# Three value turns a head instead of four, more of the feed-forward's products inside attention, and its weight tiles in two pools

## The chip, the core and the metric

The kernel runs on one core of one Trainium2 chip. The metric is the device time of one execution in microseconds (us), lower is better. An execution's profile names the engines PE (TensorE's matmuls), PEld (its weight loads, which lie beside them), DVE (VectorE), ACT (ScalarE), POOL (GpSimd) and SP (the engine that issues nearly all DMAs here).

## The reference

A block of attention and a gated feed-forward read the same x (2048 rows of 448), and a sigmoid gate per row mixes them. There are 16 heads of 28, and F is 1792.

```python
def _A_ref(x, wqkv, wo):
    qkv = (x @ wqkv).reshape(B, S, 3, H, Dh).transpose(2, 0, 3, 1, 4)
    q, k, v = qkv[0], qkv[1], qkv[2]
    scores = jnp.einsum("bhqd,bhkd->bhqk", q, k) * (Dh ** -0.5)
    p = _softmax(scores, axis=-1)
    o = jnp.einsum("bhqk,bhkd->bhqd", p, v)
    return o.transpose(0, 2, 1, 3).reshape(B, S, D) @ wo

def _B_ref(x, w_gate, w_up, w_down):
    return (_gelu(x @ w_gate) * (x @ w_up)) @ w_down

g = _sigmoid((x * gate_w).sum(-1, keepdims=True))
return g * a + (1 - g) * b
```

All is float32. A product that needs the full width is made of a high and a low part of each operand; 448 rows then take 11 matmuls of 128 rows (the list PAIRS).

## The kernel before

It has three stages, with PE's matmuls in the order in which they are written (`mm` pins each behind the one before). The other engines' instructions, DMA issues too, are ordered by a planner from its own estimate of when each is ready, except where they are pinned.

The first stage makes Q and K (tiles `pqk`, stored to `qkd`) and V with the gate column (`pv`).

**Attention** goes head by head, and in a head over 16 tiles `kt` of 128 keys. `scores` makes for each `kt` two score tiles (`half` 0 and 1): two matmuls into an `sc` tile of 1024 columns (three buffers), then one exponential on ACT into a `pt` tile (12 buffers). `values` multiplies V with the `pt` tiles of one `kt` into `po`, one PSUM bank, in column groups of 32, so that four matmuls stand side by side in the array. The values of several `kt` are done together as a turn: `ENDS` names the `kt` after which a turn's tiles are complete, and the turn's `values` follow `LATE` score tiles later. Between score tiles `fill` takes steps from the generator `up` (line 338): each step is one of the 11 matmuls of a tile `pu`, first for x @ w_up of all 14 tiles of F, then for x @ w_gate of the first `NB` tiles. A finished tile is copied by DVE (L352) to `u` and stored to `ud`. There is one `pu` bank, so after a finished tile `fill` gives nothing until `hold` is counted down by one per score tile, or a turn of values clears it. `RATE` says how many steps follow a score tile; in the first turn of the first head and the last of the last it is 4, and none follow the tile just before a turn's values. What is left at the end of the heads is done behind the last values (line 406). The weights' halves for it are loaded and split by `load_half`.

After a head's last values `finish` (line 319) copies `po` to `o`, sends its row of sums through DRAM (`dend`, `r`, `rdend`, `rb`), multiplies, and stores to `od`: four transfers one behind another, all on SP's queue.

**The last stage** goes over F in chunks of two tiles (`ORDER` lists chunks) and in each over four blocks of 512 rows (`tb`). `hidden` loads `u`, gets x @ w_gate either from DRAM (`gs`, for the first `NB` tiles of F) or by 11 matmuls `pg`, and makes the hidden tile `hl2` by gelu, product, and high and low parts on ACT and DVE. `down` multiplies the block before with w_down, 24 matmuls `pd`, and DVE adds them into `acc`. PE's order is: the `pg` of one block, then `down` of the block before it. `load_f` loads w_down's rows for one tile of F and splits them into a tile `w0`, `w1` or `w2`, in rotation (L431, L432). In chunks 2 and 3 the attention's output is loaded (`load_o`) and multiplied with wo (`project`).

On-chip memory is a stack of pools from the left, and one from the right for pools with `side="right"`. A pool that takes over memory of a closed one waits until that is free: as a whole, or tile by tile where it says `reuse_waits="tile"`. Before the change `w0`, `w1`, `w2` and `draw` lie in one pool `gp` on the right, opened ahead of attention.

Of the kernel before, what the change touches and what calls it, by code (L numbers as in the profile page):

```python
# [7 lines left out]
F32 = mybir.dt.float32  # L8
F32R = mybir.dt.float32r
# [7 lines left out]
S, D, H, DH, F = 2048, 448, 16, 28, 1792  # L17
P = 128
TB = 512
# [3 lines left out]
NQK = 2 * D // P  # L23
NF = F // P
FC = 2
ENDS = (3, 7, 11, 15)
LATE = 3
RATE = 2
NB = 3
ORDER = (2, 3, 1, 4, 0, 5, 6)  # L30
AHEAD = 8
WARM = 9
LAG = 6
# [12 lines left out]
def gated_mix(ctx: ExitStack, tc: tile.TileContext, xT, wqk, wvg, wg, wu, wd, wo, sel, ident, out):  # L46
# [12 lines left out]
    rdend = dram.tile([H, S], F32, name="rdend")  # L59
    ud = dram.tile([NF + NB, P, S], F32, name="ud")  # L60

# [22 lines left out]
    with ExitStack() as ph:  # L84
# [87 lines left out]
        def v_tile(i):  # L172
            p = psv.tile([P, VW], F32, name="pv")
            for j, (x, w) in enumerate(PAIRS):
                m = mm(p, X[:, x, i * P:(i + 1) * P], WV[:, w, :], j == 0, j == len(PAIRS) - 1)
            a = pin(nc.scalar.activation(V[:, i, :, 0:DH], p[:, 0:D].rearrange("p (h d) -> p h d", h=H), AF.Copy))
            d = pin(nc.vector.tensor_copy(gate[:, 0, i:i + 1], p[:, D:D + 1]))
            return m, a, d
# [30 lines left out]
        for i in range(4, NT):  # L209
            last = v_tile(i)  # L210
# [40 lines left out]
    with tc.If(bounded < 1, label="rows"):  # L251
        with ExitStack() as ph:
            gp = ph.enter_context(tc.tile_pool(name="gp", bufs=2))
# [23 lines left out]
                nc.sync.dma_start(out=shd[h].rearrange("a (i n) -> i a n", i=NT),  # L277
                                  in_=ms.bitcast(F32))

    gp = ctx.enter_context(tc.tile_pool(name="gp", bufs=1, side="right"))  # L280
    def by_act(o, i):
        return nc.scalar.activation(o, i, AF.Copy)


    with ExitStack() as ph:
        pp = ph.enter_context(tc.tile_pool(name="pp", bufs=12))
        op = ph.enter_context(tc.tile_pool(name="op", bufs=2))
        psc = ph.enter_context(tc.tile_pool(name="psc", bufs=3, space=PSUM))
        pso = ph.enter_context(tc.tile_pool(name="pso", bufs=1, space=PSUM))
        psu = ph.enter_context(tc.tile_pool(name="psu", bufs=1, space=PSUM))  # L290
        PT, PO = {}, {}

        def load_head(h):
            Q, K = heads[h % 2]
            if h:
                load_k(K, h)
                load_q(Q, h)
            nc.sync.dma_start(out=Q[4 * DH:NR].bitcast(F32), in_=shd[h])

        def scores(h, kt, half):  # L300
            Q, K = heads[h % 2]
            sc = psc.tile([P, 1024], F32, name="sc")
            for c in range(2):
                mm(sc[:, c * 512:(c + 1) * 512], K[:, kt * P:(kt + 1) * P],
                   Q[:, half * 1024 + c * 512:half * 1024 + (c + 1) * 512], True, True)
            pt = pp.tile([P, 1024], F32, name="pt")
            nc.scalar.activation(pt, sc, AF.Exp, scale=SCALE)  # L307
            PT[h, kt, half] = pt

        def values(h, kt):  # L310
            if kt == 0:
                PO[h] = pso.tile([P, 512], F32, name="po")
            for j in range(4):
                mm(PO[h][j * 32:(j + 1) * 32], V[:, kt, h, :],
                   PT[h, kt, j // 2][:, (j % 2) * 512:(j % 2 + 1) * 512], kt == 0, kt == NKT - 1)
            if kt == NKT - 1:
                finish(h)

        def finish(h):
            o = op.tile([P, 512], F32, name="o")  # L320
            nc.vector.tensor_copy(o, PO[h])
            for j in range(4):
                nc.sync.dma_start(out=dend[h:h + 1, j * 512:(j + 1) * 512],
                                  in_=o[j * 32 + DH:j * 32 + DH + 1])
            r = op.tile([P, S // P], F32, name="r")
            nc.sync.dma_start(out=r, in_=dend[h].rearrange("(p n) -> p n", p=P))
            nc.vector.reciprocal(r, r)
            nc.sync.dma_start(out=rdend[h].rearrange("(p n) -> p n", p=P), in_=r)
            rb = op.tile([P, 512], F32, name="rb", bufs=1)
            for j in range(4):  # L330
                nc.sync.dma_start(out=rb[j * 32:(j + 1) * 32],
                                  in_=rdend[h:h + 1, j * 512:(j + 1) * 512].to_broadcast([32, 512]))
            nc.vector.tensor_tensor(o, o, rb, OP.mult)
            for j in range(4):
                nc.sync.dma_start(out=od[h * DH:(h + 1) * DH, j * 512:(j + 1) * 512],
                                  in_=o[j * 32:j * 32 + DH])

        def up():

            todo = [(wu, f, "u") for f in range(NF)] + [(wg, f, "g") for f in range(NB)]  # L340
            for n, (_, f, key) in enumerate(todo):
                for tb in range(NTB):
                    if tb == 1 and 1 < n + 1 < len(todo):
                        load_half(*todo[n + 1], nc.vector.tensor_copy)
                    s = slice(tb * TB, (tb + 1) * TB)
                    p = psu.tile([P, TB], F32, name="pu")
                    for i, (x, w) in enumerate(PAIRS):
                        mm(p, halves[key, f][:, w], X[:, x, s], i == 0, i == len(PAIRS) - 1)
                        if i < len(PAIRS) - 1:
                            yield False  # L350
                    u = op.tile([P, TB], F32, name="u")
                    nc.vector.tensor_copy(u, p)  # L352
                    nc.sync.dma_start(out=ud[n, :, s], in_=u)
                    yield True

        filler = up()

        hold = 0

        def fill(n):  # L360

            nonlocal hold
            while n and not hold:
                n -= 1
                if next(filler, None):
                    hold = 2

        def spaced(h, kt, half):
            nonlocal hold
            scores(h, kt, half)  # L370
            hold = max(hold - 1, 0)

        def gates():

            pin(nc.scalar.activation(gate[:, 0], gate[:, 0], AF.Exp, scale=-1.0))
            nc.vector.tensor_scalar(gate[:, 0], gate[:, 0], 3e38, 1.0, OP.min, OP.add)
            nc.vector.reciprocal(gate[:, 1], gate[:, 0])
            nc.vector.tensor_scalar(gate[:, 2], gate[:, 1], -1.0, 1.0, OP.mult, OP.add)

        load_head(0)  # L380
        fill(11)
        ready, due, count = [], [], 0
        for h in range(H):
            for kt in range(NKT):
                if kt == 2 and h + 1 < H:
                    load_head(h + 1)
                if kt == 2 and h == 1:
                    gates()
                for half in range(2):
                    spaced(h, kt, half)  # L390
                    count += 1
                    if due and count == LATE:
                        for a in due:
                            values(*a)
                        due, hold = [], 0
                    elif count != LATE - 1 or h + kt == 0:
                        first, last = h == 0 and kt <= ENDS[0] + 1, h == H - 1 and kt > ENDS[-2]
                        fill(4 if first or last else RATE)
                ready.append((h, kt))
                if kt in ENDS:  # L400
                    ready, due, count = [], ready, 0
        fill(11)
        for a in due:
            values(*a)
        hold = 0
        while next(filler, None) is not None:
            pass
    attn.close()


    with ExitStack() as ph:
        ap = ph.enter_context(tc.tile_pool(name="ap", bufs=1, reuse_waits="tile"))
        acc = ap.tile([P, NT, D], F32, name="acc")
        hp = ph.enter_context(tc.tile_pool(name="hp", bufs=2, reuse_waits="tile"))
# [6 lines left out]
        def load_f(f):  # L421
            if f >= NB:
                load_half(wg, f, "g", by_act)

            n = len(WD) % 3
            size, hi, lo = ((TB + D, 0, TB), (TB + D, 0, TB), (TB + D + 32, 64, 64 + D))[n]
            w = gp.tile([P, size], F32R, name=f"w{n}", bufs=1)
            draw = gp.tile([P, D], F32, name="draw")
            nc.sync.dma_start(out=draw, in_=wd[f * P:(f + 1) * P])
            hi, lo = w[:, hi:hi + D], w[:, lo:lo + D]  # L430
            nc.scalar.activation(hi, draw, AF.Copy)  # L431
            nc.vector.tensor_tensor(lo, draw, hi.bitcast(F32), OP.subtract)  # L432
            WD[f] = hi, lo

        def hidden(f, tb, hl):
# [3 lines left out]
            g = tp.tile([P, TB], F32, name="g")  # L439
            if f < NB:  # L440
                pg = tp.tile([P, TB], F32, name="gs")
# [62 lines left out]
                    mm(p, O[:, x, i * P:(i + 1) * P], WO[:, w], k == 0, k == len(PAIRS) - 1)  # L504
                nc.vector.scalar_tensor_tensor(acc[:, t], p, gate[:, 1, t:t + 1], acc[:, t], OP.mult, OP.add)

        order = [f for c in ORDER for f in range(c * FC, (c + 1) * FC)]
        load_f(order[0])
        pend = None
        for n in range(NF // FC):  # L510
# [53 lines left out]
```

## Time and profile before

| | |
|---|---|
| median of 3 runs | 1052.24 us (1051.49 to 1052.64) |
| the profiled execution | 1051.69 us |
| its span, first to last instruction | 1049.9 us |
| PE busy in the span | 1041.3 us (99%) |
| ACT busy | 610.5 us (58%) |
| DVE busy | 315.7 us (30%) |
| granted TensorE clock, mean | 1.000 |

The span is what the page and the trace divide up; the rest of the profiled execution lies around it. A line of the timeline gives the start in us, the duration, the engine, the source line and the operation as out<-in, with a count where equal instructions are merged; in square brackets stands the idle time before it and what ended it. All matmuls carry line 52, that of the helper `mm`, so they are told apart by their tiles. A matmul of `po` counts as two instructions. Matmuls are pipelined and a duration reaches into the next one's, so what one costs PE is read from start to start.

### The profile page before, as it was taken

Reading aid. Unit: us, or ns where it says so; the run is one execution under the profiler, and the core shown is the slowest. Engines: PE = TensorE matmul, PEld = TensorE weight load, DVE = VectorE, ACT = ScalarE, POOL = GpSimd, SP = SyncE. Lnnn points to the kernel's source line nnn. Section 1 sums busy time; section 2 is a strip of 40 time slices with the busy share of each in tenths; the row PEclk is TensorE's granted clock in tenths of the full one; section 3 lists DMA queues with packets and bytes.
Section 4 is the critical chain, followed back from the end, with each engine's and each line's share of the span. In section 5 each row is a group of like instructions: output and inputs, shape, how many; then the busy total and the mean of one; then the engine's idle time right before and its main releaser. Section 6 shows DMA issues by size and latency. Waiting matters only on the chain.

```text
span 1049.9 us, 14556 instructions
## 1 busy us (share of the span) xinstructions
PE 1041.3 (99%) x5673; PEld 731.4 (70%) x5673; DVE 315.7 (30%) x512; ACT 610.5 (58%) x732; POOL 51.3 (5%) x38
## 2 busy tenths in 40 slices
PE   9999999999999999999999999999999999999998
PEld 6889765655655656656556556556588898899887
DVE  4552112111111011011011111110157666577555
ACT  5332477877777778778777777787643332233321
POOL 4322000000000000000000000000001011100000
PEclk9999999999999999999999999999999999999999
DMA  7865333332332332332332332331264323242223
GB/s 250 306 253 122 79 94 87 118 104 80 108 95 77 111 95 75 108 101 74 104 105 75 98 110 74 96 109 37 70 190 141 112 80 100 88 150 68 67 86 117
DMA packets 58906, 115.84 MB, mean 110 GB/s; under 512 B 12784, under 2 KB 18160, under 8 KB 55216
## 3 DMA queue, kind: packets, MB, share of 16 engines
q1 hardware_dynamic: 58544, 114.32, 36.2%
q8 instruction: 47, 0.77, 0.3%
q10 hardware_dynamic: 288, 0.52, 0.2%
q14 instruction: 27, 0.22, 0.1%
HBM read 74.44 MB, written 40.37 MB: 109 GB/s over the span
## 4 chain that ended last, share of the span: by engine, by line
PE 88%; ACT 0%; issue 0%; DVE 0%; ACTq 0%
PE sc L52 23%; PE po L52 22%; PE pd L52 16%; PE pu L52 16%; PE pg L52 11%; ACT pt L307 0%; DVE y L470 0%; ACT w L431 0%; ACTq L307 0%
## 5 line engine op out<-in xcount | busy, mean ns | idle before, releaser
L307 ACT ACTIVATE pt<-sc 128x1024 f32<-128x1024 f32 x512 | 477.9, 1040 | 160.7 <-PE sc L52 160.4
L52 PE MATMUL sc<-Q,K 128*128 128x512 f32 x1024 | 313.5, 398 | 1.7 <-issue 1.6
L52 PEld LDWEIGHTS sc<-Q,K 128*128 128x128 f32 x1024 | 187.1, 188 | 91.0 <-issue 54.8
L52 PE MATMUL pu<-X,half 128*128 128x512 f32 x748 | 233.3, 391 | 0.1
L52 PE MATMUL po<-pt,V 128*32 128x512 f32 x2048 | 233.0, 595 | 0.0
L352 DVE COPY u<-pu 128x512 f32<-128x512 f32 x68 | 47.0, 691 | 488.3 <-PE pu L52 477.4
L52 PEld LDWEIGHTS pu<-X,half 128*128 128x128 f32 x748 | 140.1, 188 | 32.4 <-issue 1.4
L52 PEld LDWEIGHTS po<-pt,V 128*32 128x32 f32 x2048 | 60.0, 109 | 138.2 <-issue 132.7
L52 PE MATMUL pd<-w,hl 128*128 128x448 f32 x672 | 140.1, 365 | 0.0
L52 PEld LDWEIGHTS pd<-w,hl 128*128 128x128 f32 x672 | 126.2, 188 | 11.1
L52 PE MATMUL pg<-X,half 128*128 128x512 f32 x484 | 114.0, 390 | 0.0
L52 PEld LDWEIGHTS pg<-X,half 128*128 128x128 f32 x484 | 90.9, 188 | 18.4
L52 PE MATMUL pqk<-X,WQK 128*128 128x512 f32 x308 | 70.9, 391 | 1.0 <-ACT X L143 0.8
L52 PEld LDWEIGHTS pqk<-X,WQK 128*128 128x128 f32 x308 | 57.5, 188 | 14.7 <-ACT X L143 1.5
L447 ACT ACTIVATE g<-pg 128x512 f32<-128x512 f32 x44 | 26.2, 594 | 70.3 <-PE pg L52 70.2
L448 DVE TENSOR_TENSOR g<-g,u 128x512 f32<-128x512 f32 x56 | 46.4, 837 | 50.8 <-ACT g L447 50.7
L449 ACT ACTIVATE hl<-g 128x512 fp32r<-128x512 f32 x56 | 35.2, 631 | 42.2 <-DVE g L448 36.8
L467 DVE SCALAR_TENSOR_TENSOR acc<-pd,gate,acc 128x448 f32<-128x448 f32 x80 | 52.7, 679 | 6.0 <-PE pd L52 5.9
L495 POOL TENSOR_TENSOR ohl<-oraw,ohl 128x1536 fp32r<-128x1536 f32 x4 | 14.0, 3502 | 704.8 <-ACT ohl L491 704.8
L450 DVE TENSOR_TENSOR hl<-g,hl 128x512 fp32r<-128x512 f32 x56 | 38.3, 687 | 10.6 <-ACT hl L449 8.5
L162 ACT ACTIVATE hl<-pqk 128x512 fp32r<-128x512 f32 x28 | 16.7, 598 | 41.6 <-PE pqk L52 39.7
L52 PE MATMUL pv<-WV,X 128*128 128x450 f32 x176 | 36.5, 367 | 0.0
(62 smaller groups left out, 357.0 us busy)
## 6 DMA issues: line engine op xcount, KB each, us to landing
ud<-u SPq DMA_DIRECT2D x68, 256.0 KB
qkd<-hl SPq DMA_DIRECT2D x28, 512.0 KB
K<-qkd SPq DMA_DIRECT2D x64, 224.0 KB
Q<-qkd SPq DMA_DIRECT2D x64, 224.0 KB
u<-ud SPq DMA_DIRECT2D x56, 256.0 KB
rb<-rdend SPq DMA_DIRECT2D x64, 64.0 KB
raw<-in_xT SPq DMA_DIRECT2D x14, 256.0 KB
hraw<-in_wu SPq DMA_DIRECT2D x14, 256.0 KB
```

Of the source, the lines that this page charges most:

```text
L52: return pin(nc.tensor.matmul(o, lhsT, rhs, start=start, stop=stop))
L162: pin(nc.scalar.activation(hl[:, 0], p, AF.Copy))
L307: nc.scalar.activation(pt, sc, AF.Exp, scale=SCALE)
L352: nc.vector.tensor_copy(u, p)
L447: nc.scalar.activation(g, pg, AF.Gelu_apprx_tanh)
L448: nc.vector.tensor_tensor(g, g, u, OP.mult)
L449: nc.scalar.activation(hl[:, 0], g, AF.Copy)
L450: nc.vector.tensor_tensor(hl[:, 1], g, hl[:, 0].bitcast(F32), OP.subtract)
L467: nc.vector.scalar_tensor_tensor(acc[:, t], p, g1, acc[:, t], OP.mult, OP.add)
L495: nc.gpsimd.tensor_tensor(O[:, 4:7], o[:, 0:3], O[:, 0:3].bitcast(F32), OP.subtract)
```

## The change

`ENDS` has three turns a head, of 5, 5 and 6 key tiles, instead of four of 4. `LATE` is 2: a turn's values follow the second score tile behind its end. `RATES` replaces `RATE`, two filler steps for the first six score tiles of a turn and three for the next six, and the tile before the values is no longer left without. `HOLD` counts three score tiles instead of two. `NB` is 6: x @ w_gate of six tiles of F is made in attention, so 20 x 44 filler matmuls instead of 17 x 44. `ORDER` lists tiles instead of chunks: the first chunk has two computed tiles (6, 7), and each of the others one computed and one loaded. There are 14 `pt` tiles and one `o`. `gp` becomes `gp0`, with `w0` and `draw`, and a new pool `gp1` on the right, opened with the last stage, with `w1` and `w2`; the two halves of a weight tile lie at 0 and at 512 in each.

```diff
-ENDS = (3, 7, 11, 15)
-LATE = 3
-RATE = 2
-NB = 3
-ORDER = (2, 3, 1, 4, 0, 5, 6)
+ENDS = (4, 9, 15)
+LATE = 2
+RATES = (2,) * 6 + (3,) * 6
+HOLD = 3
+NB = 6
+ORDER = (6, 7, 8, 0, 9, 1, 10, 2, 11, 3, 12, 4, 13, 5)
...
-    gp = ctx.enter_context(tc.tile_pool(name="gp", bufs=1, side="right"))
+    gp0 = ctx.enter_context(tc.tile_pool(name="gp0", bufs=1, side="right"))
...
-        pp = ph.enter_context(tc.tile_pool(name="pp", bufs=12))
+        pp = ph.enter_context(tc.tile_pool(name="pp", bufs=14))
...
-            o = op.tile([P, 512], F32, name="o")
+            o = op.tile([P, 512], F32, name="o", bufs=1)
...
                 if next(filler, None):
-                    hold = 2
+                    hold = HOLD
...
-                    elif count != LATE - 1 or h + kt == 0:
+                    else:
                         first, last = h == 0 and kt <= ENDS[0] + 1, h == H - 1 and kt > ENDS[-2]
-                        fill(4 if first or last else RATE)
+                        fill(4 if first or last else RATES[count - 1])
...
     with ExitStack() as ph:
+        gp1 = ph.enter_context(tc.tile_pool(name="gp1", bufs=1, side="right"))
         ap = ph.enter_context(tc.tile_pool(name="ap", bufs=1, reuse_waits="tile"))
...
             n = len(WD) % 3
-            size, hi, lo = ((TB + D, 0, TB), (TB + D, 0, TB), (TB + D + 32, 64, 64 + D))[n]
-            w = gp.tile([P, size], F32R, name=f"w{n}", bufs=1)
-            draw = gp.tile([P, D], F32, name="draw")
+            w = (gp1 if n else gp0).tile([P, 2 * TB if n else TB + D + 32], F32R, name=f"w{n}")
+            draw = gp0.tile([P, D], F32, name="draw")
             nc.sync.dma_start(out=draw, in_=wd[f * P:(f + 1) * P])
-            hi, lo = w[:, hi:hi + D], w[:, lo:lo + D]
+            hi, lo = w[:, 0:D], w[:, TB:TB + D]
...
-        order = [f for c in ORDER for f in range(c * FC, (c + 1) * FC)]
+        order = ORDER
```

## The prediction

> **What bounds the kernel now.** I read the page's busy times first, then its chain of work that ended last.
>
> ```profile
> span 1049.9 us, 14556 instructions
> PE 1041.3 (99%) x5673; PEld 731.4 (70%) x5673; DVE 315.7 (30%) x512; ACT 610.5 (58%) x732; POOL 51.3 (5%) x38
> PE sc L52 23%; PE po L52 22%; PE pd L52 16%; PE pu L52 16%; PE pg L52 11%; ACT pt L307 0%; DVE y L470 0%; ACT w L431 0%; ACTq L307 0%
> ```
>
> PE is busy all the time, and the chain is PE from end to end. A change pays only if it takes time from PE's own stream, and costs whatever it leaves PE waiting. So next comes one turn of attention from the timeline (start, duration, engine, line), and busy time by stretch (PE, PEld, DVE, ACT, POOL, granted clock, DMA share, GB/s) for all of attention and for a stretch of the last stage.
>
> ```profile
> 298.84 3.64 PE L52 MATMUL po<-pt,V 128*32 128x512 f32 x32
> 299.29 0.13 PEld L52 LDWEIGHTS po<-pt,V 128*32 128x32 f32 x4 [0.30 <-issue]
> ...
> 301.44 0.13 PEld L52 LDWEIGHTS po<-pt,V 128*32 128x32 f32 x4 [0.30 <-issue]
> 302.41 0.73 PE L52 MATMUL sc<-Q,K 128*128 128x512 f32 x2
> 302.98 0.62 PE L52 MATMUL pu<-X,half 128*128 128x512 f32 x2
> ...
> 307.76 1.08 PE L52 MATMUL sc<-Q,K 128*128 128x512 f32 x4
> 308.77 1.07 PE L52 MATMUL po<-pt,V 128*32 128x512 f32 x8
> ```
>
> ```profile
> 135.00:735.00 600.00, 599.93 (x3558) 358.60 (x3557) 81.19 (x141) 452.57 (x491) 0.00 (x0) 1.00 0.32 92
> 838.00:880.00 42.00, 42.00 (x203) 37.89 (x203) 26.85 (x41) 11.96 (x19) 4.11 (x2) 1.00 0.39 115
> ```
>
> From one po block's start to the next are 9.93 us: 3.57 us of values, then 16 score and 11 pu matmuls. In both stretches PE waits for nobody.
>
> **The turns.** Between 302.98 and 307.76 lie 21 matmuls (11 pu, 10 sc), 0.2276 us each. The first two of the turn take 302.98 - 302.41 = 0.57 us, 0.115 more than 2 x 0.2276. The last four take 308.77 - 307.76 = 1.01 us, 0.10 too much. The values go in eight groups of (301.44 - 299.29) / 5 = 0.43 us, so 3.44 us, and the block lasts 3.57, 0.13 more. One turn thus costs about 0.345 us that is no matmul's own. The change makes 3 turns a head of 4, 48 of 64 in all: 16 x 0.345 = **-5.5 us**. The bounds are nothing, if the 0.345 goes with the value steps, which stay the same in number, and 5.5. I take 5.5, since it sits only at the two seams and both remain as they were.
>
> The Trainium skill (TensorEngine Tiling, Key Properties) says that changing the tiling mode drains TensorE; po runs as 128*32 and the rest as 128*128, and the row's seams agree.
>
> **What the longer turns ask.** Followed through the loop, a turn between values is S uu S uu S uu S uu S uuu S S S, then S with two or three u behind it (S a score tile of two matmuls, u one pu matmul). Up to the eighth S this is the old turn within one matmul, so ACT meets it as before. Its rate and its lag:
>
> ```profile
> 739.47 0.73 PE L52 MATMUL sc<-Q,K 128*128 128x512 f32 x2
> 740.30 7.45 ACT L307 ACTIVATE pt<-sc 128x1024 f32<-128x1024 f32 x8 [1.98 <-PE sc L52]
> L307 ACT ACTIVATE pt<-sc 128x1024 f32<-128x1024 f32 x512 | 477.9, 1040 | 160.7 <-PE sc L52 160.4
> L352 DVE COPY u<-pu 128x512 f32<-128x512 f32 x68 | 47.0, 691 | 488.3 <-PE pu L52 477.4 <-DMA ud<-u 6.8 <-DVEq L251 4.0
> ```
>
> An exponential follows the last by (7.45 - 1.04) / 7 = 0.916 us, and the first starts 0.83 us after its tile. The seventh ends at 0.83 + 6 x 0.916 + 1.04 and 0.2 of waiting for the sixth tile, which has 21 matmuls before it: 7.6 us. The tenth tile, which needs its buffer, starts at 34.5 x 0.2276 = 7.9 us. It fits with 0.3 us to spare: cost nothing, and if it is late it costs the lateness on each of 48 turns. Six steps need 12 pt tiles and two more before the values: the 14 that there are. One psu bank lies idle while DVE copies it (0.69 us); HOLD keeps two or three score tiles over that, or one and the values. One o buffer is enough, since its use below lasts some 24 us of a head's 42 (4 x 9.93, less one seam, and 11 matmuls more).
>
> **The moved products.** Three more tiles of x @ w_gate are 3 x 4 x 11 = 132 matmuls. In attention they cost 0.2276 us, in the last stage 0.228 (9.97 us for 44 below): nothing. Around them go 12 copies of 0.69 us and three weight splits on DVE (81 of 600 us busy in attention), 12 stores and 12 loads of 256 KB more on SP's queue (DMA share 0.32 and 0.39). In the last stage each block of 512 rows has then one pg tile (2.5 us) instead of two. The row 838 to 880 is that case already: one tile computed, one loaded, and PE ran 42.00 of 42.00 us. DVE worked 26.85 of them, so it would need half as much again to become the bound.
>
> **The end of attention.** All 20 x 44 = 880 filler matmuls are used up before the end: behind the values of the last middle turn come S uuuu S uuuu S uuu and then seven S with nothing between, and no filler behind the last values. Three psc buffers let PE run three tiles ahead. The fourth S starts at 19.5 x 0.2276 = 4.4 us, its exponential at 4.7, the seventh tile's at 7.45, and the tenth S waits for that to end at 8.5; it ends at 9.05. Unhindered it would end at 31.5 x 0.2276 = 7.2. So +1.9 us; before, the same stretch (749.41 to 757.06, 7.65 us for 32 matmuls and seams, 7.50) lost 0.15: **+1.7 us**.
>
> **The weights of the second tile.** Here is the step that decides. Before, w0, w1 and w2 had memory of their own through attention:
>
> ```profile
> L431 ACT ACTIVATE w<-draw x14: 562/579/637, 161.2 to 1010.5; 128x448 fp32r<-128x448 f32 x14
> L432 DVE TENSOR_TENSOR w<-draw,w x14: 614/624/626, 161.8 to 1011.1; 128x448 fp32r<-128x448 f32 x14
> 757.06 3.64 PE L52 MATMUL po<-pt,V 128*32 128x512 f32 x32
> 760.63 2.79 PE L52 MATMUL pu<-X,half 128*128 128x512 f32 x11
> 760.77 0.69 DVE L321 COPY o<-po 128x512 f32<-128x512 f32 x1 [2.91 <-PE po L52]
> 761.49 1.12 SPq L323 DMA_DIRECT2D dend<-o  x4
> 763.26 10.14 PE L52 MATMUL pg<-X,half 128*128 128x512 f32 x44
> 765.66 0.32 SPq L326 DMA_DIRECT2D r<-dend  x1
> 769.97 0.33 SPq L328 DMA_DIRECT2D rdend<-r  x1
> 773.23 5.03 PE L52 MATMUL pd<-w,hl 128*128 128x448 f32 x24
> 773.32 1.71 SPq L331 DMA_DIRECT2D rb<-rdend  x4
> 779.26 0.68 DVE L333 TENSOR_TENSOR o<-o,rb 128x512 f32<-128x512 f32 x1
> 779.97 1.65 SPq L335 DMA_DIRECT2D od<-o  x4
> 784.56 0.49 SPq L488 DMA_DIRECT2D oraw<-od  x1
> ```
>
> The first split ran at 161 us. After the change only w0 is there early; w1 and w2 lie in gp1, opened after attention on the right, below gp0. Per partition the left side then reaches 57,568 (keep) + 16,384 (fw) + 32,768 (V) + 32,768 (Q, K) + 57,344 (14 pt) + 8,320 (op) = 205,152 bytes, and gp0 with gp1 takes 13,952 from the top. The kernel before fills 212,448. If that is about all there is, gp1 lies on op's u, o, r and rb, and w1 can't be written until finish(15) is done with them. The two stay apart only if there are 219,104 bytes.
>
> The Trainium skill (SBUF — State Buffer, "SBUF size: 192, 224, or 256?") gives about 208 KiB usable on trn2, 212,992 bytes; no run here shows it, and by it they overlap.
>
> finish(15) took from 760.63, when its values ended, to 784.56, when the first load that needs its store was let go: 23.9 us. PE's first down product stands behind 44 pg matmuls (9.97 us) and reads w1 at its fourth matmul, 0.6 us on: 10.6 us after the values, since no filler lies between them any more. What delayed r before was that filler's store; ACT's and DVE's work hangs on the pg tiles, which come 2.6 us earlier. So the chain shifts to 21.3 us, w1's first half follows 0.6 later (579 ns), and PE waits 21.9 - 10.6 = 11.3 us. Without anything ahead of it in a queue it would be shorter, with the gap from rdend to rb in another head as the landing of each small transfer:
>
> ```profile
> 719.75 0.69 DVE L321 COPY o<-po 128x512 f32<-128x512 f32 x1 [3.83 <-PE po L52]
> 722.51 0.34 SPq L326 DMA_DIRECT2D r<-dend  x1
> 726.32 0.37 SPq L328 DMA_DIRECT2D rdend<-r  x1
> 728.24 1.71 SPq L331 DMA_DIRECT2D rb<-rdend  x4
> ```
>
> r is issued 2.8 us after the copy, and four more landings at 1.9 with the issues of rb and od (1.7, 1.6), DVE's two steps (0.9) and w1's copy (0.6) come to 15.3 us: a wait of 4.7. The upper bound is before's chain unshifted, 24.5 - 10.6 = 14. I take **+10 us**, near the row that is this very chain. Behind the waiting matmul stand all others of PE's queue; ACT and DVE wait for their pg tiles, so nothing is caught up. On ACT the copy into w1 waits too, with the gelus of later tiles behind it; the first four tiles' are ready long before, and I take them as queued ahead of it.
>
> **PE after the rest.** No row shows PE after a rest of 10 us within the kernel. After 1.6 us it loses nothing; from the start of the program it is slow:
>
> ```profile
> 1.47 4.21 PE L52 MATMUL warm<-zero 128*128 128x512 f32 x9 [1.47 <-DVE zero L100]
> 119.12 1.16 PE L52 MATMUL sc<-Q,K 128*128 128x512 f32 x4 [1.62 <-issue]
> 120.14 1.19 PE L52 MATMUL pu<-X,half 128*128 128x512 f32 x4
> ```
>
> Nine matmuls in 4.21 us, against 9 x 0.228 = 2.05. Bounds 0 and 2.2; I take **+2**, since a rest of 10 us is nearer to the first row.
>
> The Trainium skill (TensorE: Matmul & The Clock Gate, Part 1) has the clock at half after an idle window of about 3.4 us and until as long a busy one, which would be some 1.7 us, an estimate; the granted clock in this trace is 1.00 everywhere.
>
> **The sum.** -5.5 + 1.7 + 10 + 2 = +8.2 us. The profiled execution took 1051.69 us (span 1049.9, 1.8 around it), so 1059.9; the median shown is 0.5 above it. I say 1060, with 1052.5 to 1064 for this case from its bounds (wait 4.7 or 14, clock 0 or 2.2).
>
> **Rivals.** *The weights come in time*: gp1 lies free, or w1 is ready within 10.6 us of the last values. Then 1051.7 - 5.5 + 1.7 = 1048, faster. For it: the four landings are short taken singly. Against: the bytes, and the 23.9 us. It decides at 10.6. *The turns save nothing*: the seam's time goes with the value steps; with the wait it is 1065.4, without it 1053.4. Against: the seam stands at the mode's change alone. *Late score tiles*: the exponentials fall behind by 0.1 us more than the 0.3 on every turn, 48 x 0.1 = 5 us on top, 1065.
>
> **Chances.** The wait with the saving 0.64; weights in time 0.22; no saving, with the wait 0.05, without 0.03; late score tiles 0.06. A measurement here tells 0.2%, 2 us, from no change. Of the first case 0.05 falls within 0.2%, with the 0.03 that makes 0.08 for the same, 0.22 faster and 0.70 slower. The range, 1047.5 to 1065, takes in the second case and leaves out the ends beyond the bounds.
>
> **What would show it.** Right: 48 po blocks with the same seams; seven S in pace with ACT before the last; no w of the second tile before op's last store; PE idle 4.7 to 14 us ahead of the fourth pd matmul, released by the split of w. Wrong: an early split of the second w, or pd following pg without a gap; sc waiting for pt on middle turns; PE idle in the last stage's blocks.

## The result, and the profile after

The changed kernel is slower: 1082.38 us, median of 4 runs (1081.75 to 1084.36), against 1051.97 us for the kernel before in the same session (4 runs, 1051.49 to 1052.64). The ratio is 1.029, 95% interval 1.0278 to 1.0302. The forecast was 1060 with a range of 1047.5 to 1065: the sign was right, the size was not.

First the head of the page after, and its chain of work that ended last by engine.

```profile
span 1080.0 us, 14639 instructions
PE 1043.3 (97%) x5673; PEld 735.5 (68%) x5673; DVE 321.0 (30%) x527; ACT 607.8 (56%) x729; POOL 51.0 (5%) x38
...
PE 84%; DMA 2%; DVE 1%; SPq 1%; issue 1%; ACT 0%; DVEq 0%; ACTq 0%
```

Before, the chain was PE from end to end and PE was busy 99% of the span. Now DMA, DVE and SP's queue have entered the chain. PE executes as many matmuls (5673) and is busy only 2.0 us longer, so nearly all of the 30.1 us more span is time in which it stands. The waits of PE (line, releaser: us in total, times, longest) say where:

```profile
PE pd L53 <- ACT w L433: 15.9, 1, 15.9
PE pu L53 <- DVE u L354: 8.8, 3, 3.1
PE pd L53 <- DVE w L434: 2.5, 1, 2.5
...
PE sc L53 <- ACT pt L309: 1.1, 4, 0.6
```

Two kinds of stop were in no row of before: one of 15.9 + 2.5 = 18.4 us at the first down product, which the prediction had foreseen at 10, and three of about 3 us at filler matmuls, which it had not.

The start of the first pg divides the two stages. The timeline of after, around that place:

```profile
801.79 10.27 PE L53 MATMUL pg<-X,half 128*128 128x512 f32 x44
801.92 0.69 DVE L323 COPY o<-po 128x512 f32<-128x512 f32 x1 [9.07 <-PE po L53]
...
807.79 0.32 SPq L328 DMA_DIRECT2D r<-dend  x1
...
811.13 0.33 SPq L330 DMA_DIRECT2D rdend<-r  x1
...
811.89 0.77 PE L53 MATMUL pd<-w,hl 128*128 128x448 f32 x3
...
817.76 1.71 SPq L333 DMA_DIRECT2D rb<-rdend  x4
819.26 2.03 DVE L483 TENSOR_TENSOR WO<-oraw,WO 128x1792 fp32r<-128x1792 f32 x1 [4.23 <-ACT WO L482]
...
821.25 0.69 DVE L335 TENSOR_TENSOR o<-o,rb 128x512 f32<-128x512 f32 x1
821.31 0.38 SPq L488 DMA_DIRECT2D oraw<-od  x1
821.97 1.61 SPq L337 DMA_DIRECT2D od<-o  x4
826.52 1.48 ACT L493 ACTIVATE ohl<-oraw 128x1536 fp32r<-128x1536 f32 x1 [7.29 <-DMA oraw<-od]
...
827.91 0.56 ACT L433 ACTIVATE w<-draw 128x448 fp32r<-128x448 f32 x1
828.13 3.43 POOL L497 TENSOR_TENSOR ohl<-oraw,ohl 128x1536 fp32r<-128x1536 f32 x1 [743.39 <-ACT ohl L493]
828.50 3.55 DVE L434 TENSOR_TENSOR w<-draw,w 128x448 fp32r<-128x448 f32 x1 [6.55 <-ACT w L433]
828.52 1.11 PE L53 MATMUL pd<-w,hl 128*128 128x448 f32 x2 [15.86 <-ACT w L433]
...
832.10 6.43 PE L53 MATMUL pd<-w,hl 128*128 128x448 f32 x19 [2.47 <-DVE w L434]
...
838.37 5.18 PE L53 MATMUL pg<-X,half 128*128 128x512 f32 x22
```

Up to pg the kernel takes 801.79 - 763.26 = 38.5 us more than before. The moved products are 132 x 0.2276 = 30.0 of these, so attention itself has become **8.5 us** slower. From pg to the end it takes 1080.0 - 801.8 = 278.2 us, against 1049.9 - 763.3 = 286.6 less the 30.1 that moved away, 256.5: **21.7 us** slower. The two together are the 30.1, within rounding.

The three-turn schedule itself is visible: blocks of x40, x40 and x48 po instructions a head. At the end of attention come seven score tiles in ACT's pace, as predicted (seven exponentials in 6.51 us from 792.03). The long stop is also where it was predicted: the fourth down matmul waits for the copy of w, and that copy starts only after op's last store. By the profile's chain of work, the last part of that store is issued at 823.20 and lands 4.03 us later, and what releases ACT's copy of w is this landing. But the chain that leads to it (o, dend, r, rdend, rb, o, od, w) takes 26.7 us, from the end of the values at 801.8 to the first half of w at 827.91 + 0.56 = 828.5; the prediction had 21.9. And the three stops within attention are new.

This is one of them, in the timeline of after (PE's other matmuls left out):

```profile
309.17 0.43 DVE L80 CAST half<-hraw 128x512 fp32r<-128x512 f32 x1 [4.64 <-PE pu L53]
...
310.24 0.68 DVE L335 TENSOR_TENSOR o<-o,rb 128x512 f32<-128x512 f32 x1
310.95 1.60 SPq L337 DMA_DIRECT2D od<-o  x4
312.59 0.39 SPq L241 DMA_DIRECT2D Q<-qkd  x1
...
313.33 0.82 SPq L355 DMA_DIRECT2D ud<-u  x2
...
317.03 0.69 DVE L354 COPY u<-pu 128x512 f32<-128x512 f32 x1 [6.11 <-DMA ud<-u]
...
317.78 0.75 PE L53 MATMUL pu<-X,half 128*128 128x512 f32 x2 [3.10 <-DVE u L354]
```

Read it from the bottom. PE waits for the copy of pu, since there is one pu bank. The copy waits for a store of u: there are two u buffers. That store stands on SP's queue behind the stores of od. Those wait for the product of o and rb on DVE, and this stands on DVE behind the split of the next weight half (L80), which waits 4.64 us for PE to read the old half for the last time. Nobody needs that split soon. It is only ahead in the queue.

### The profile page after: what moved, and what is told of

It is laid out like the page before. It is cut to its first block, busy times and chain, and to the rows that moved or that the text cites. A ratio compares the mean times of both kernels' runs of the same rounds, so it can differ in the third digit from the quotient of the medians.

```text
span 1080.0 us, 14639 instructions
## 1 busy us (share of the span) xinstructions
PE 1043.3 (97%) x5673; PEld 735.5 (68%) x5673; DVE 321.0 (30%) x527; ACT 607.8 (56%) x729; POOL 51.0 (5%) x38
## 4 chain that ended last, share of the span: by engine, by line
PE 84%; DMA 2%; DVE 1%; SPq 1%; issue 1%; ACT 0%; DVEq 0%; ACTq 0%
PE sc L53 22%; PE po L53 20%; PE pu L53 19%; PE pd L53 16%; PE pg L53 7%; DMA ud<-u 1%; DMA oraw<-in_wo 1%; SPq L337 1%; DMA od<-o 0%; DVE w L434 0%; DVE o L335 0%; DVE u L354 0%; ACT pt L309 0%; DVE WO L483 0%; ACT WO L482 0%
## 5 line engine op out<-in xcount | busy, mean ns | idle before, releaser
L53 PE MATMUL sc<-Q,K 128*128 128x512 f32 x1024 | 308.3, 398 | 2.6 <-issue 1.5
L53 PE MATMUL pu<-X,half 128*128 128x512 f32 x880 | 260.6, 392 | 9.0 <-DVE u L354 8.8
L53 PE MATMUL po<-pt,V 128*32 128x512 f32 x2048 | 229.7, 594 | 0.0
L354 DVE COPY u<-pu 128x512 f32<-128x512 f32 x80 | 55.3, 692 | 485.0 <-PE pu L53 397.9
L53 PEld LDWEIGHTS pu<-X,half 128*128 128x128 f32 x880 | 165.5, 188 | 46.3 <-DVE u L354 10.1
L53 PE MATMUL pd<-w,hl 128*128 128x448 f32 x672 | 143.9, 370 | 18.3 <-ACT w L433 15.9
L53 PEld LDWEIGHTS pd<-w,hl 128*128 128x128 f32 x672 | 128.2, 191 | 30.9 <-ACT w L433 16.2
L53 PE MATMUL pg<-X,half 128*128 128x512 f32 x352 | 85.0, 391 | 0.0
L449 ACT ACTIVATE g<-pg 128x512 f32<-128x512 f32 x32 | 19.1, 597 | 109.3 <-PE pg L53 109.3
L53 PEld LDWEIGHTS pg<-X,half 128*128 128x128 f32 x352 | 66.0, 188 | 14.0 <-issue 0.8
L450 DVE TENSOR_TENSOR g<-g,u 128x512 f32<-128x512 f32 x56 | 41.8, 782 | 54.8 <-ACT g L449 54.8
L163 ACT ACTIVATE hl<-pqk 128x512 fp32r<-128x512 f32 x28 | 16.7, 598 | 40.4 <-PE pqk L53 38.5
```

The source lines that it names most:

```text
L53: return pin(nc.tensor.matmul(o, lhsT, rhs, start=start, stop=stop))
L163: pin(nc.scalar.activation(hl[:, 0], p, AF.Copy))
L449: nc.scalar.activation(g, pg, AF.Gelu_apprx_tanh)
L450: nc.vector.tensor_tensor(g, g, u, OP.mult)
```

## The experiments

The theory after the result names two independent causes, w1's place in memory (about 21 us) and the order of DVE's queue in attention (about 11 us). Without both, the change should be worth what it was forecast to bring without the wait. Rivals: the long turns or the moved products cost time by themselves, or one cause is a consequence of the other.

**gp1 on the left.** Then w1 and w2 no longer lie on op's memory.

```diff
-        gp1 = ph.enter_context(tc.tile_pool(name="gp1", bufs=1, side="right"))
+        gp1 = ph.enter_context(tc.tile_pool(name="gp1", bufs=1))
```

> The changed kernel with gp1 opened on the left, over V's old place, which is free as soon as the last values are done. Theory 'weights wait for memory': of the changed kernel's 30 us, 21.6 stand between the first pd matmul (811.9) and the end of its block (838.4, 26.5 us where 4.9 are work). They go: 1082.4 - 21.6 = 1061, and pd follows pg without a gap. Rival 'something else of the last stage is late' (the hidden tiles, wo's load, finish's own chain on ACT and DVE): the gap stays at 10 us or more, 1072 or above.

1061.66 us (1059.45 to 1067.21), 20.7 less than the change; ratio to before 1.009 (1.0068 to 1.0111). The profile is of the slowest of its four runs. PE's waits in it:

```profile
PE pu L53 <- DVE u L354: 8.4, 3, 3.0
...
PE pd L53 <- ACT w L433: 1.1, 1, 1.1
```

The long wait is gone, the three stops remain. Its last stage takes 1065.4 - 807.1 = 258.3 us instead of 278.2.

**The halves held in place.** The load and the two splits of the next half are pinned where they are written, behind the first tile of the current half.

```diff
-                        load_half(*todo[n + 1], nc.vector.tensor_copy)
+                        load_half(*todo[n + 1], nc.vector.tensor_copy, pin)
```

> The changed kernel with the filler's weight loads and splits (hraw, half) kept in the written order on SP and DVE, so that DVE doesn't stand before a split whose buffer PE still reads. Theory 'early split': the split held back the product o x rb on DVE, that held the store od on SP, and od held the stores ud behind it, for which u's copy waited; PE stood still three times, 3.3 + 1.5 (half clock) + 2.8 + 3.2 = 10.8 us. They go: 1082.4 - 10.8 = 1071.5. Rival 'too many transfers' (five u tiles a head in two u buffers and one o buffer are too much for SP's queue, whatever DVE's order): the three stops stay, 1080 or above.

1069.93 us (1069.69 to 1070.63), 12.4 less than the change; ratio to before 1.0178 (1.0161 to 1.0195). In PE's waits no pu is left, and w's are nearly as they were:

```profile
PE pd L53 <- ACT w L433: 14.6, 1, 14.6
PE pd L53 <- DVE w L434: 2.5, 1, 2.5
```

Its pg starts at 790.42, 11.4 us ahead of the changed kernel's: that is what the three stops cost there.

**Both remedies.**

> Both edits together. Theory: both losses go, 1082.4 - 21.6 - 10.8 = 1050, so just below the kernel before (1052), by the seams' 5.5 us less 1.7 at the end of attention and 1.3 in small waits of the score tiles. Rival 'the losses stand for one another' (what one edit frees, the other then waits for): 1056 or more.

1050.87 us (10 runs, 1049.03 to 1052.67); ratio 0.9993 (0.9983 to 1.0002), no difference to before. The two remedies took 20.7 and 12.4 us one at a time, 33.1, and 31.5 together. Since the runs with gp1 on the left are spread over 8 us, the stages of the profiles say it more firmly than these sums: with gp1 on the left alone only the last stage is shorter (258.3 us, and 258.2 with both), with the halves held alone only attention is (pg at 790.42, and at 790.35 with both; its last stage still takes 1067.9 - 790.4 = 277.5). The causes are independent, and together they are the whole loss. In this kernel's timeline a head with nothing in its way runs as follows:

```profile
686.81 4.50 PE L53 MATMUL po<-pt,V 128*32 128x512 f32 x40
701.89 5.36 PE L53 MATMUL po<-pt,V 128*32 128x512 f32 x48
715.61 4.50 PE L53 MATMUL po<-pt,V 128*32 128x512 f32 x40
728.77 4.50 PE L53 MATMUL po<-pt,V 128*32 128x512 f32 x40
```

That is 41.96 us a head. Before it was 4 x 9.93 = 39.72, and 11 filler matmuls more are 2.50: 42.22. So a head gains 0.26 us, and 16 heads 4.2.

**Which of the pinned instructions mattered.** Only DVE's splits are held, the loads on SP are left to the planner, and gp1 is on the left.

```diff
-                        load_half(*todo[n + 1], nc.vector.tensor_copy)
+                        load_half(*todo[n + 1], nc.vector.tensor_copy, lambda i: i if i.ins.engine == nc.sync.engine else pin(i))
```

> The changed kernel with gp1 on the left and only DVE's splits of the next weight half held to their written place; the halves' loads stay where the planner puts them on SP. If the split ahead of the product o x rb on DVE is what stops PE three times, the stops go as they did with everything held: about 1051. If it was the place of the load on SP, they stay: about 1061.

1051.29 us (1050.22 to 1053.31), ratio 0.9994 (0.9984 to 1.0003): the order on DVE alone is the cause. Its timeline at the place shown above:

```profile
303.80 0.69 DVE L354 COPY u<-pu 128x512 f32<-128x512 f32 x1 [9.89 <-PE pu L53]
304.41 0.68 DVE L335 TENSOR_TENSOR o<-o,rb 128x512 f32<-128x512 f32 x1
305.01 0.42 DVE L80 CAST half<-hraw 128x512 fp32r<-128x512 f32 x1
305.12 1.59 SPq L337 DMA_DIRECT2D od<-o  x4
```

The product of o and rb comes 5.8 us earlier, od with it, and the split, now behind it, waits for nothing.

**gp1 tile by tile.** Does w1 itself lie on what finish(15) uses, or does it only wait because the pool is taken over as a whole?

```diff
-        gp1 = ph.enter_context(tc.tile_pool(name="gp1", bufs=1, side="right"))
+        gp1 = ph.enter_context(tc.tile_pool(name="gp1", bufs=1, side="right", reuse_waits="tile"))
```

> The changed kernel with gp1 on the right as it is, but taking its memory over tile by tile instead of as a whole pool. If w1 itself lies on o, r, rb, the wait for the second w_down tile stays: about 1082. If only the whole-pool wait is at fault (w1 lies on u or nothing that is in use so late), the 21 us go: about 1061.

1085.51 us (1077.13 to 1085.88), ratio 1.0312 (1.0296 to 1.0328). The wait for w stays, and in this profile's chain, too, the landing of od's last store comes directly before the copy of w. So the tile itself lies on memory that is used to the end:

```profile
PE pd L53 <- ACT w L433: 14.9, 1, 14.9
PE pu L53 <- DVE u L354: 7.8, 3, 2.9
```

Its runs are spread over 9 us, as those of the kernel with gp1 on the left were over 8; the profile is of the fastest of its five. The three stops cost different amounts in different executions. The window from 300 to 345 us around the first stop, in the profile of gp1 on the left and then in this one (busy us of PE, PEld, DVE, ACT, POOL, granted clock, DMA share, GB/s):

```profile
300.00:345.00 45.00, 42.01 (x224) 26.73 (x217) 6.03 (x10) 27.63 (x30) 0.00 (x0) 0.92 0.27 81
```

```profile
300.00:345.00 45.00, 42.11 (x251) 25.80 (x247) 6.03 (x10) 30.01 (x32) 0.00 (x0) 1.00 0.31 89
```

PE is busy as long in both, but at a granted clock of 0.92 in the first. Against pg's start in the kernel with both remedies (790.35) the three stops cost 807.08 - 790.35 = 16.7 us in the first, and 798.96 - 790.35 = 8.6 in the second.

**More turns.** The saving by fewer turns was worked out from two seams in one row. Here the kernel before gets twice as many turns, with the same matmuls.

```diff
-ENDS = (3, 7, 11, 15)
+ENDS = (1, 3, 5, 7, 9, 11, 13, 15)
...
-RATE = 2
+RATE = 3
```

> The kernel before with eight value turns a head (behind every second key tile) instead of four, and three filler steps behind a score tile instead of two so that as much filler goes in: the same matmuls, 64 turns more. Theory: a turn costs PE 0.345 us at its two seams, whatever number of values it holds: 64 x 0.345 = +22 us, about 1074. Rival: the time goes with the value steps, which stay the same in number: 1052.

1080.40 us (1080.16 to 1080.66), ratio 1.0268 (1.0252 to 1.0284): 28.7 us for 64 turns, 0.45 each. Its turns in the timeline:

```profile
296.48 1.92 PE L52 MATMUL po<-pt,V 128*32 128x512 f32 x16
...
306.84 1.92 PE L52 MATMUL po<-pt,V 128*32 128x512 f32 x16
```

Two turns take 10.36 us, for 16 score and 11 pu matmuls (27 x 0.2276 = 6.15) and 8 groups of values (8 x 0.43 = 3.44). That leaves 0.77, 0.385 a turn; 128 such turns against 64 of 0.345 make 27.2 of the 28.7. The rival, that the time goes with the value steps, is out: their number did not change.

**A fuller end, three times.** The last seven score tiles lose about 2 us to ACT because no filler is left. First attempt, on top of both remedies: fewer filler steps in all heads, so that some are left at the end, and HOLD back at 2.

```diff
-RATES = (2,) * 6 + (3,) * 6
-HOLD = 3
+RATES = (2,) * 8 + (3, 3, 2, 2)
+HOLD = 2
```

> Both edits, and RATES (2 x 8, 3, 3, 2, 2) with HOLD 2, so that two filler tiles are left behind the last values and four steps stand behind each of the last score tiles. Theory: the 1.8 us that PE lost beside the last seven exponentials go, 1048 to 1048.5. Rival: the end of attention costs nothing there since PE waits later anyway, 1050 as with both edits alone.

1070.64 us (1069.17 to 1071.44), ratio 1.0177 (1.016 to 1.0194), 19.8 us slower than with both remedies alone. In the waits of its weight loads the filler now comes too soon behind the copy of pu:

```profile
PEld pu L53 <- DVE u L354: 30.1, 66, 2.8
```

With these rates two score tiles do not cover that copy, in the kernel before they did (3 such waits, 0.9 us). Both constants were changed at once here, and HOLD 2 with the change's own rates was not run. Second attempt: HOLD 3 again, and fewer steps in the last two heads alone.

```diff
-                        fill(4 if first or last else RATES[count - 1])
+                        fill(4 if first or last else 2 if h >= H - 2 else RATES[count - 1])
```

> The changed kernel with both remedies (gp1 on the left, the halves' loads and splits held to their written place), and in the last two heads two filler steps behind every score tile instead of two and three, so that filler is left for the last turn. Theory: the 1.8 us that the last seven score tiles lose to ACT go, about 1049 (1050.9 less 1.8). Rival: the end of attention is not what the last stage's start waits for, or the exponentials fall behind elsewhere: 1051.

1050.37 us (11 runs, 1048.78 to 1054.05), ratio 0.999 (0.998 to 1.0): not to be told from before, nor from the kernel with both remedies. PE's waits for pt at the end are gone, yet its pg starts at 790.31 instead of 790.35. Head 14 has 12 filler matmuls fewer; 7 of them, 1.59 us, are missing between the two blocks shown here, but the time between them is only 41.96 - 41.03 = 0.93 us shorter:

```profile
686.97 4.50 PE L53 MATMUL po<-pt,V 128*32 128x512 f32 x40
...
728.00 4.50 PE L53 MATMUL po<-pt,V 128*32 128x512 f32 x40
```

What is saved at the end is lost where it is taken from. The likely reason is that a long turn needs its filler to give ACT time: in these two heads (690 to 770 us) the weight loads of score tiles wait 4.0 us for ACT, where they wait 1.0 in the kernel with both remedies. Third attempt: take the filler from the last stage instead, with a seventh tile of x @ w_gate in attention.

```diff
-NB = 6
-ORDER = (6, 7, 8, 0, 9, 1, 10, 2, 11, 3, 12, 4, 13, 5)
+NB = 7
+ORDER = (7, 0, 8, 1, 9, 2, 10, 3, 11, 4, 12, 5, 13, 6)
```

> The changed kernel with both remedies and x @ w_gate of seven tiles in attention instead of six, every chunk of the last stage with one computed and one loaded tile: the same matmuls in all, but filler behind the last turn's score tiles and 33 matmuls left behind the last values. Theory: PE no longer waits for ACT at the end of attention (-1.8 us) without thinning any other turn, and the last values' chain gets 7.5 us of cover (-1 us, the wait for w left in the run with both remedies): about 1048. Rival: what the end gives is lost again at the start of the last stage, where one pg tile now stands ahead of the first down product instead of two: 1051.

1054.47 us (1052.73 to 1062.79), ratio 1.0034 (1.0016 to 1.0051): 2.8 us slower than before, and beyond the rival's 1051. What the rival said of the place holds: the end of attention no longer waits, but PE now waits at the tiles left behind the last values and at the first down product:

```profile
PE pu L53 <- DVE u L354: 1.6, 2, 0.8
...
PE pd L53 <- DVE w L434: 1.2, 1, 1.2
PE pd L53 <- ACT hl L451: 1.2, 1, 1.2
```

No kernel here beats the one before by more than a measurement can tell.

## Why the prediction was right or wrong

**The turns, -5.5.** The mechanism was right: time goes with the number of turns. Its size was 4.2 us, by the head above. A long turn costs 0.38 us ((41.96 - 55 x 0.2276 - 64 x 0.2276 - 16 x 0.86) / 3 = 0.37, with 0.86 for the eight matmuls of a key tile's values), not 0.345; why the long ones cost a little more was not tried. The term was the sum of two seams in a turn of four key tiles, and the seams were taken as the same in any turn; they are 0.385 in turns of two.

**The end of attention, +1.7.** Right. In the kernel with both remedies the last turn takes 13.92 us (its po blocks start at 771.15 and 785.07) for 31 matmuls (7.06) and five key tiles' values (4.30); less 0.37 for the seams it loses 2.2, where 1.9 was forecast, against 0.15 before: +2.0 for the 1.7.

**"The moved products: nothing."** This step failed. The matmuls cost what was forecast (44 in 9.97 us are 0.2266 each rather than 0.228, 0.2 us on the 132), and in the last stage PE was busy 200.00 of 200 us from 860 to 1060. But "12 copies, 12 stores and 12 loads" were weighed by their duration and by how busy DVE (81 of 600 us) and SP were, and that says nothing about what stands behind what. The extra filler gives five u tiles a head where there were four, while a weight half still serves four. So the split of the next half meets the end of a head at a different place each time, and three times the planner put it ahead of the product of o and rb. A 0.43 us instruction that waits 4.64 us then holds up od, Q, the stores of u and in the end PE: 11.4 us in all in this execution. That the order on DVE is the cause is shown. That the count of five against four makes the place rotate is read from the loop and was not tried by itself; the rows fit it, since the three splits stand 172.8 and 170.8 us apart (309.17, 482.00, 652.77), about four heads, after which five and four meet again.

**"One o buffer is enough", "14 pt tiles fit", HOLD.** These held. The copy to o (L323) is released by PE's values, not by the tile; PE waits for pt four times in all, in the last turn; and with HOLD 3 the filler's weight loads wait for the copy of u three times only, at the three stops (66 times in the run with HOLD 2, which had other rates too).

**The weights, +10, and the clock, +2.** The mechanism was right in each step: w1 lies on memory that op uses to the end, its copy follows op's last store, the wait sits at the fourth down matmul, and it goes with the memory. The size was wrong: 18.4 us of waiting instead of 10, outside the bounds of 4.7 and 14. The clock's term was about right: the 19 matmuls behind the wait take 838.37 - 832.10 = 6.27 us, where 24 take 5.03 before, so 2.3 us too many, and the granted clock from 828 to 834 us is 0.50. The remaining 1.0 of the 21.7 has the size of what the kernel with both remedies keeps too (258.2 - 256.5 = 1.7, with a wait of 1.0 for the next w).

The step that failed here is the length of the chain, from the last values to the first half of w: 26.7 us instead of 21.9. The prediction shifted before's by 2.6 us, because "ACT's and DVE's work hangs on the pg tiles, which come 2.6 us earlier". **That shift did not come:** rdend left 9.34 us behind the values before (769.97 - 760.63) and after (811.13 - 801.79). r had stood behind the filler's store before; now it stands on SP behind a load of u that waits for DVE's product on a pg tile, and goes 6.0 us behind the values where it was 5.0.

Then rb goes 6.6 us after rdend, where it was 3.4 before: **3.3 us more**. The 8 KB of rdend are on their way with wo's load (896 KB), two of u and one of gs around them. The DMA view of the stretch from 811 to 823 us shows the engines full until about 817 (busy share in tenths, 0.3 us a digit):

```profile
DMA  6797799999999999988410000027453695771355
```

DVE's product follows rb after 3.5 us, 2.4 less than the 5.9 before, directly behind the split of wo (2.03 us); whether it also waited for that split the trace does not say. From od's first store to the landing of its last part are 5.25 us, where the prediction had counted 4.6, from 779.97 to 784.56, to the first load that the store releases; a load of attention output (768 KB, L488) goes out just ahead of it. That is 0.7 more. ACT's copy into w then begins 0.7 us after the landing, behind a copy of ohl of 1.48 us that had started at 826.52. In sum 2.6 + 3.3 - 2.4 + 0.7 + 0.7 = 4.9 for the 4.8 that the chain is too long.

The rest lies behind the chain and in no term: DVE's half of w took 3.55 us instead of 0.62, beside POOL, and that is PE's second wait of 2.5 us. And the 10 was itself 1.3 less than the 11.3 that the shifted chain gave. The wait for w1 was priced as a chain of transfers, with what else stands in those queues at the new time left out. That each piece adds its time is read from the rows and was not tried one by one.

**The sum again.** With the measured sizes it is -4.2 + 2.0 + 11.4 + 18.4 + 2.3 + 1.0 = 30.9, against 30.1 in the spans; most of the 0.8 between them lies in attention (9.2 for the measured 8.5) and stays open. The first two terms were within 1.3 us of the forecast. The miss is the 11.4 that was put at nothing and the 8.4 more of the wait.

**The rival "weights in time", 1048.** With both remedies the kernel does what that rival says, and takes 1050.87: the saving of 5.5 was 4.2, and the last stage keeps 1.7 us that the sum had not.

## What to carry to other kernels

Before pricing moved work by its duration, list for every in-order queue what will stand behind each of its waiting instructions: a split of 0.43 us cost 11.4 us by its place. Memory given back late holds work up like a data dependency: before a pool is opened on the far side of the stack, see which tile it will lie on and when that tile's last reader ends. And saved seams are only worth having where the other engine (here ACT, 0.916 us a score tile) still gets its time between them.

## What the runs showed of the hardware

A DVE operation with two inputs that began while POOL ran its subtraction ended only after it: 828.50 + 3.55 = 832.05, against POOL's 828.13 + 3.43 = 831.56, for an operation whose other occurrences take 0.62. It was no single case: in the kernel before, a product of 0.69 us took 2.46 us or more beside each of POOL's four subtractions. The Trainium skill (SBUF — State Buffer, "SBUF: two separate sides") says that a DVE operation with two SBUF inputs and a GpSimd operation that reads SBUF exclude each other for the whole instruction; these rows agree.

A rest of PE of about 3 us was enough to halve its rate in some executions and not in others. In the kernel with gp1 on the left the first stop shows a granted clock of 0.92 over 45 us, and these rows behind the wait, 0.85 us for two matmuls instead of 0.455:

```profile
318.96 1.22 PE L53 MATMUL pu<-X,half 128*128 128x512 f32 x2 [2.99 <-DVE u L354]
319.98 1.05 PE L53 MATMUL sc<-Q,K 128*128 128x512 f32 x2
320.83 1.05 PE L53 MATMUL pu<-X,half 128*128 128x512 f32 x2
...
325.10 0.67 PE L53 MATMUL sc<-Q,K 128*128 128x512 f32 x2
```

The half rate lasts 6.1 us there. In the kernel that takes gp1 over tile by tile, after a rest of the same kind, the clock stays at 1.00. The spread of such kernels goes with the clock: the four runs with gp1 on the left took 1067.21, 1063.84, 1059.48 and 1059.45 us at mean granted clocks of 0.992, 0.995, 1.000 and 0.999. A clock lower by 0.008 is 8.5 us of 1065, most of what lies between one execution and the next. The granted clock does not show every slow stretch: in the kernel before it reads 1.00 from 1.47 to 5.70 us, where the program's first nine matmuls took 4.21 us instead of 2.05.
